# Half-array tiles for the second MLP product, four strips for the KV product, one half-array pair for the memory readout, in an infini-attention and mixer-MLP kernel

## The chip, the cores and the metric

The kernel runs on one core of one Trainium2 chip. The time is device microseconds of one execution of the whole program. TensorE (PE in the profile) multiplies and writes the accumulators in PSUM, which has eight banks; VectorE (DVE) and ScalarE (ACT) read them; GpSimd (POOL) works on SBUF alone; SyncE (SP) issues most of the DMAs.

## The reference

Two branches read the same normalised input and are added to it. With `x` of 2048 tokens by 512 features, 32 heads of 16, four segments of 512 tokens, and an MLP of 1792 hidden features:

```
xn = layernorm(x)
q, k, v = xn@wq, xn@wk, xn@wv              # 32 heads, 4 segments s
for s in segments:
    p     = softmax(q_s k_s^T * scale + mask)   # mask: -1e9 for keys after the query
    a_dot = p v_s
    a_mem = (phi(q_s) M) / (phi(q_s) z + 1e-6)  # phi(t) = t+1 or exp(t)
    o_s   = g*a_mem + (1-g)*a_dot               # g = sigmoid(beta), one per head
    M += phi(k_s)^T v_s ;  z += sum over tokens of phi(k_s)
out = x + o@wo + ( gelu(layernorm(xn)@w1 + b1)@w2 + b2 )
```

## The kernel before

The attention runs in 16 units `i`: four segments `s` by four groups `g` of eight heads (128 features). The MLP runs in 16 jobs `j`: eight blocks of 256 tokens (`hf`) by two halves of the hidden features (`fh`, `FH` = 7 chunks of 128). Most products are split into fp16 high and low parts, so that three fp16 matmuls stand for one (`split3`, L457, and the loops at L757 and L776). Every step is a key such as `("M", i, n)`; `streams()` lists the keys of each kind in their own order, and the string `ORDER` gives, letter by letter, from which list the next key is taken. Nothing reorders afterwards: each engine works through its instructions in that order, and an instruction whose semaphores are not there yet holds up what stands behind it on its engine. So `ORDER`, a table written out by hand or by a program, sets what lies between what.

The steps that matter here, with the lines that the profile shows:

- `T` (`qk_proj`, L457): projects q or k of one unit; the result goes through DRAM (`qd`, `kd`) into `qst`, `kst`, where heads lie on 48 rows from partitions 0 and 64.
- `M` (`m_jobs`, L580): q k^T for the row maxima; each step issues matmuls in pairs, one on array rows 0 to 47 and one on rows 64 to 111, into two PSUM banks. DVE takes the maxima (L587). There are 12 steps in a unit.
- `S` (`s_jobs`, L620): the logits again, transposed, in pairs on 50 rows each; ACT takes the exponent (L625), POOL masks (L634).
- `pv`, `PV` (`pv`, L649): fp32 probabilities times values, in four strips of 32 array columns that run side by side.
- `K` (`kv`, L556): phi(k)^T v, four fp32 products of 128 by 128, then masked to the heads' own blocks into `mst` (DVE L559, L563; POOL L564); the sum `z` comes from an accumulator output of L494 into `zst` (L561).
- `Z`, `Qd`, `Q` (`z_rep`, `a_mem`): L520 spreads `z`; one fp32 product for the denominators (L528), a reciprocal by ACT and DVE (L530, L507, L508, L512, L513), one fp32 product for the numerators (L536), multiplied in L537.
- `D` (`d_jobs`, L457), `G`, `H`: the first MLP product, GELU, and the split of the hidden part into `hT`.
- `e`, `E` (`e_jobs`, L757): the second MLP product. For each of two blocks `a` of 128 tokens, seven chunks of three full 128x128 fp16 matmuls add up in the bank `eacc`; then DVE adds the bank to `acc` (L761).
- `out` (L776, L779): the product with `wo`.

PSUM is divided in two: seven banks that all steps share (`dps`, tile `dense`) and one for `eacc` (`eps`). A transpose (L442, L501, L595) uses a shared bank too.

The array stands in one of three tilings in this program: full (128 rows by 128 columns), two halves of 64 rows (`M` and `S`), and four strips of 32 columns (`pv`). Read along PE's instructions, the tiling changes 412 times.

Of the kernel before, what the change touches and what calls it, by code (L numbers as in the profile page):

```python
# [57 lines left out]
def streams():  # L58
# [47 lines left out]
    "aacactutacttuaeuuutcccavecevvvaatcvcctvbwwvactwdvvwwftvttvxtxxbvytcxbvtwxcgcbxwxywxxhooobycxxsgycoiyziyizyonyo"  # L106
    "ciiyzzoypniizpniApifpnAqziqiiqqqzAzoimzzAzoozpoAoosjijqijjiqsjjioAiikkckkbihijqjsijijcqjiijqbqiqpfkbqkkakpmAAA"
    "ojAlqgjljojjqajlhookkkAkipiojopisjjiqjijqjipqiBqqiiBiAfoaqiikkkBkqqpqipgqmqspqlBphoqjljmjojiqiajqliojsiaikakkk"
    "ipiBqaqqjjjqoqjooajiqajioaisiibqfbpqkkkkqibqplqqpbgBpqhqlqmojjoqjjoojlioijiqkkipkkiBqjijqojijqqjjioqiipkkkkBli"
    "ifmnilnmlnbgrjjrjbjsrjijqqipiniikskkkipqqjijrjjiqjoiiqjikkkpkmlmioolhiofmqqoqpsjjmqjjgjjlqookbkkkmmsbjijijqqij"  # L110
    "ijiojiskikkkoplqiqholaiiifqmioqpomiqspgpqopqqaqqajjjqqomjiqjijqliqaqiikkipkkopiaajipshqoqijqjijpqijqqijaqopiqk"
    "kkaklqqomaoloaqqjbjfmoqbjsjjlqqmjbgkkkkbmmjjqojjqojiiojopibikkpkkpiiolnpiilhnqiiifqmilnompibngrjmjjjrjjsohipik"
    "kkskipirmjijrjiqjijqijqqqiipkkkkliiqqosqlqoiflomqoopqjjmsqjjgjjoombkkpkkqbqjmjiiqjqjijiqisjqqpsipkkkkiqqliqlho"
    "qqiiaifqmioomiqplgoqppmsaaoqjjjsqqomqjijqiqjiaoikikpakkqipqjiqqijqajoajjjohqqiikkkkpoalipiqqlooiaooaqbpmfqlbjm"
    "jjjqqjjqgbkkkkmbjjjqqoojibjqimjpqqqiikkkkplibiqolfinqiipnliimnpiomiogrojjmjsrjjoiipnjiqiikskkkiirjijqqijqjijqi"
    "jripkkkkiplqplfsqqoolqqmqojjjqmjjgojomkpkkksojqjjijqijiqiqpqjiosisikkpkqkbqlqilfisqqbiiiqpqmooipomqmgqqojjojjq"
    "ojqjliiiikkkkpijpoijiqjjiqjiijqikkiqpsqikkpqqqplplooqojqjjojjqqjlmokkkkqpqjjqjjqoojqjpqqkkkkqqplmqqqqqpqppqqqq"
    "lqqqqlqqqqrrqrr"
# [3 lines left out]
def plan():  # L122
# [3 lines left out]
    for c in "".join(ORDER):  # L126
        key = next(todo[NAMES.index(c)])
        k = key[0]
        need = "G" if k == "G" else "E" if k in ("S", "Qd") or k == "O" and key[2] == 0 or k == "T" and (
            key[1] >= NG if key[2] == 0 else key[1] < NU - NG) else tab  # L130
        yield key, None if need == tab else need
        tab = need
# [3 lines left out]
def infini_mixer_kernel(ctx: ExitStack, tc: tile.TileContext, x, wq, wk, wv, wo, beta, w1, b1, w2, b2, out):  # L136
# [9 lines left out]
    dps = ctx.enter_context(tc.tile_pool(name="dps", bufs=7, space=PSUM))  # L146
    eps = ctx.enter_context(tc.tile_pool(name="eps", bufs=1, space=PSUM))
# [315 lines left out]
    mst = cst.tile([P, NG, P], F32, name="mst")  # L463
    zst = cst.tile([P, NG], F32, name="zst")
    zs = {}

    def qk_proj(i, which):
# [19 lines left out]
        if phi:  # L487
            V.tensor_scalar(e, e, 1.0, qkcol(3, 1 - which, g), op0=OP.min, op1=OP.mult)
            if which == 0:
                V.scalar_tensor_tensor(e, p, 0.0, e, op0=OP.max, op1=OP.add)  # L490
            else:
                if s:
                    zs[i] = sm.tile([P, 1], F32, name="zs")
                V.scalar_tensor_tensor(e, p, 0.0, e, op0=OP.max, op1=OP.add,  # L494
                                       accum_out=zs[i] if s else zst[:, g:g + 1])
# [21 lines left out]
    def z_rep(i):  # L517
        g = i % NG
        zrt[i] = sm.tile([P, P], F32, name="zr", bufs=1)
        V.tensor_scalar(zrt[i], bd.rearrange("p a b -> p (a b)"), zst[:, g:g + 1], None, op0=OP.mult)  # L520
# [3 lines left out]
    def a_mem(i, part):  # L524
        g = i % NG
        p = dense()
        if part == 0:
            T.matmul(p, zrt[i], pqt[i, 0], start=True, stop=True)  # L528
            rd = sb.tile([P, 512], F32, name="rc")
            A.activation(rd, p, AF.Copy, bias=1e-6, scale=qkcs[:, 0, g:g + 1])  # L530
            ame[i] = sb.tile([P, 512], F32, name="ame")
            log_recip(rd, ame[i])
            newton(rd, rd, ame[i])
            rden[i] = rd
        else:
            T.matmul(p, mst[:, g, :], pqt[i, 0], start=True, stop=True)  # L536
            V.scalar_tensor_tensor(ame[i], p, bg[:, g, 4:5], rden[i], op0=OP.mult, op1=OP.mult)  # L537
# [13 lines left out]
    def kv(i):  # L551
        s, g = divmod(i, NG)
        p = dense()
        for b in range(4):
            v = vt[s, b][:, 4 * g:4 * g + 4, :].rearrange("p a (b c) -> p a b c", b=3)[:, :, 0:3:2, :]
            T.matmul(p[:, :P], pkn[i][:, b, :], v, start=b == 0, stop=b == 3)  # L556
        m = bd.rearrange("p a b -> p (a b)")
        if s == 0:
            V.tensor_tensor(mst[:, g, :], p[:, :P], m, op=OP.mult)  # L559
            return  # L560
        V.tensor_tensor(zst[:, g:g + 1], zs[i], zst[:, g:g + 1], op=OP.add)  # L561
        zr = sm.tile([P, P], F32, name="zr", bufs=1)
        V.tensor_tensor(zr, p[:, :P], m, op=OP.mult)  # L563
# [312 lines left out]
```

## Time and profile before

| | |
|---|---|
| median of 3 runs | 771.83 us (767.83 to 774.05) |
| span of the profiled execution | 772.1 us |
| busy: PE, DVE, ACT, POOL | 735.6, 541.2, 528.1, 352.3 us |
| second MLP product (L757) | 672 matmuls, 174.1 us busy |
| memory readout (L528, L536) | 48 fp32 matmul passes, 25.1 us busy |
| KV product (L556) | 96 fp32 matmul passes, 13.3 us busy |

The profiled execution lies within the range of the timed runs. A busy share is an average over the start, where weights are loaded and split, a long middle, and a tail with the last MLP block and the output product. An fp32 matmul shows as two passes in the trace. In the trace's rows in order of time, neighbouring instructions of one line are merged: the first number is the start, the second the length, which for PE includes the time that the last result needs to run out of the array; so the time that PE is held by a row is the start of the next row less its own.

### The profile page before, as it was taken

What the parts mean: (1) busy time and instruction counts of PE and PEld (TensorE: products, weight loads), DVE (VectorE), ACT (ScalarE), POOL (GpSimd) and SP (SyncE); (2) the same over time, 40 slices, a digit from 0 to 9 for tenths busy, and PEclk for the clock granted to TensorE, in tenths of its full rate; (3) what the DMA queues carried; (4) which work ended last, traced back from release to release, by engine and by line L of the source; (5) the groups of instructions that cost most, each with busy time, mean ns of one, the idle gap of its engine ahead of it and who ended that gap; (6) DMA issues with size and microseconds to landing.
All of it is one profiled execution on the core that took longest, in us unless ns stands there. A gap on an engine that the chain in (4) does not pass through costs nothing.

```text
span 772.1 us, 14761 instructions
## 1 busy us (share of the span) xinstructions
PE 735.6 (95%) x5301; PEld 384.0 (50%) x5301; DVE 541.2 (70%) x1677; ACT 528.1 (68%) x908; POOL 352.3 (46%) x544
## 2 busy tenths in 40 slices
PE   5889999999999998999999999999999999999997
PEld 4653545455544454555554454454554444453543
DVE  5788868879684857899486675979567673958332
ACT  5878788776885567576873948657784578666960
POOL 4465646544523533445544444354534244334651
PEclk9999999999999999999999999999999999998999
DMA  6874314142204223211312315140221314230001
GB/s 202 248 226 138 104 38 103 44 97 62 65 7 132 56 58 97 56 56 44 90 49 53 86 53 127 35 91 29 71 70 42 97 35 105 48 78 16 2 1 55
DMA packets 54085, 59.17 MB, mean 77 GB/s; under 512 B 5038, under 2 KB 40892, under 8 KB 54012
## 3 DMA queue, kind: packets, MB, share of 16 engines
q1 hardware_dynamic: 51708, 54.04, 24.8%
q0 software_dynamic: 2304, 4.20, 3.5%
q8 instruction: 41, 0.67, 0.4%
q14 instruction: 32, 0.26, 0.1%
HBM read 41.18 MB, written 17.04 MB: 75 GB/s over the span
## 4 chain that ended last, share of the span: by engine, by line
PE 69%; DMA 11%; ACT 8%; DVE 7%; issue 3%; POOL 2%; SPq 1%; ACTq 0%; DVEq 0%; POOLq 0%
PE dense L457 27%; PE eacc L757 15%; PE dense L649 8%; PE dense L580 5%; PE dense L776 4%; PE dense L620 4%; DMA qd<-hl 4%; DMA qst<-qd 4%; ACT pt L625 3%; PE dense L528 1%; PE dense L442 1%; DVE dense L587 1%; DMA w2s<-in_B_w_dram 1%; DVE hl L479 1%; ACT hl L475 1%
## 5 line engine op out<-in xcount | busy, mean ns | idle before, releaser
L587 DVE CUSTOM_DVE_ANT_0 dense<-dense,mask 128x512 f32<-128x512 f32 (+3 forms) x512 | 241.2, 515 | 24.3 <-PE dense L580 17.8
L625 ACT ACTIVATE pt<-dense,qkcs 128x512 f32<-128x512 f32 (+1 forms) x384 | 203.8, 627 | 30.6 <-PE dense L620 28.6
L757 PE MATMUL eacc<-w2s,hT 128*128 128x512 f16 x672 | 174.1, 385 | 2.0 <-DVE acc L761 1.9
L457 PE MATMUL dense<-yT,w1s 128*128 128x256 f16 x1344 | 162.4, 273 | 4.3 <-DVE yT L446 2.9
L634 POOL TENSOR_SCALAR_AFFINE_SELECT pt<-pt 128x256 f32<-128x256 f32 x256 | 101.4, 421 | 130.1 <-ACT pt L625 129.5
L457 PEld LDWEIGHTS <-w1s 128*128 128x128 f16 x1344 | 128.5, 98 | 36.5 <-issue 11.4
L730 POOL TENSOR_TENSOR hT<-hh,hT 128x512 f16<-128x512 f32 x64 | 66.5, 1039 | 90.0 <-ACT hT L729 87.2
L757 PEld LDWEIGHTS <-hT 128*128 128x128 f16 x672 | 58.0, 98 | 80.0 <-issue 31.7
L649 PE MATMUL dense<-pt,vt 128*32 128x512 f32 (+3 forms) x1024 | 78.0, 439 | 0.7 <-POOL hh L728 0.5
L580 PE MATMUL dense<-kst,qst 48*128 48x512 f16 (+3 forms) x512 | 66.9, 305 | 8.1 <-DMA qst<-qd 5.2
L587 DVE DVE_READ_ACCUMULATOR2_ANT mc<- 128x1 f32 x512 | 72.1, 141 | 0.0
L479 DVE SCALAR_TENSOR_TENSOR hl<-dense,hl 128x512 f16<-128x512 f32 x32 | 22.1, 689 | 65.3 <-ACT phq L478 41.5
L620 PE MATMUL dense<-qst,kst 50*128 50x512 f16 (+3 forms) x512 | 64.4, 302 | 2.7 <-ACT pt L625 2.0
L728 POOL TENSOR_SCALAR hh<-hT,sc 128x512 f32<-128x512 f32 x64 | 42.8, 669 | 36.3 <-ACT hT L721 34.2
L729 ACT ACTIVATE hT<-hh 128x512 f16<-128x512 f32 x64 | 36.6, 572 | 32.5 <-POOL hh L728 32.4
L714 ACT ACTIVATE hT<-dense,b1t,sc 128x256 f32<-128x256 f32 x64 | 36.2, 566 | 23.8 <-PE dense L457 23.2
L649 PEld LDWEIGHTS dense<-pt,vt 128*32 128x32 f32 x1024 | 29.6, 110 | 44.7 <-issue 34.4
L580 PEld LDWEIGHTS <-qst 48*128 48x128 f16 x512 | 22.1, 95 | 51.9 <-issue 36.1
L475 ACT ACTIVATE hl<-dense 128x512 f16<-128x512 f32 x32 | 19.0, 595 | 41.4 <-PE dense L457 41.4
L679 POOL TENSOR_TENSOR nN<-nN,oT 128x512 f32<-128x512 f32 x16 | 20.3, 1269 | 56.9 <-DVE oT L513 56.9
L620 PEld LDWEIGHTS <-kst 50*128 50x128 f16 x512 | 21.4, 94 | 46.8 <-issue 39.8
L457 PE MATMUL dense<-xnT,wks 128*128 128x512 f16 x192 | 44.3, 379 | 0.4 <-DVE xnT L446 0.3
(225 smaller groups left out, 1034.9 us busy)
## 6 DMA issues: line engine op xcount, KB each, us to landing
xt<-in_A_x_dram SPq DMA_DIRECT2D x30, 256.0 KB
kd<-hl SPq DMA_DIRECT2D x48, 128.0 KB
kst<-kd SPq DMA_DIRECT2D x32, 192.0 KB
qd<-hl SPq DMA_DIRECT2D x48, 128.0 KB
qst<-qd SPq DMA_DIRECT2D x32, 192.0 KB
acc<-in_A_x_dram SPq DMA_DIRECT2D x16, 256.0 KB
acc<-in_B_b_dram POOLq DMA_DIRECT2D x16, 256.0 KB, 4.4
out_dram<-acc SPq DMA_DIRECT2D x16, 256.0 KB
```

Of the source, the lines that this page charges most:

```text
L457: T.matmul(p, wsl(ws, k, a), xsl(xs, k, b), start=s0 and i == 0, stop=s1 and i == 3 * n - 1)
L580: T.matmul(p[:, o:o + n], stk[i, 0][r, t, P * qb:P * qb + P], stk[i, 1][r, t, :n], start=True, stop=True)
L587: V.tensor_tensor_reduce(p[:, o:o + n], p[:, o:o + n], mask[:, 512 - n:], 1.0, -3e38, OP.add, OP.max, mc[i][:, 4 * b + t, qb:qb + 1])
L620: T.matmul(p[:, o:o + n], stk[i, 1][r, t, P * kb:P * kb + P], stk[i, 0][r, t, P * kb:], start=True, stop=True)
L625: A.activation(e[:, OFF[kbs[0]]:OFF[kbs[0]] + o], p[:, :o], AF.Exp, scale=qkcs[:, 1, i % NG:i % NG + 1])
L634: G.affine_select(v, v, pattern=[[0, 2], [1, P]], compare_op=OP.is_ge, fill=0.0, base=0, channel_multiplier=-1)
L649: T.matmul(p[32 * c:32 * c + 32, P * kb:], vt[s, kb][:, 4 * g + c, 16 * odd:16 * odd + 32], pt[i, 2 * c + odd][:, OFF[kb]:OFF[kb] + LEN[kb ...
L714: A.activation(hz[:, fi, :], p[:, :256], AF.Identity, bias=b1t[:, fo:fo + 1], scale=col(CG + fh))
L728: G.tensor_scalar(t, hz[:, z, :], col(SHH + j % 2), 0.0, op0=OP.mult, op1=OP.add)
L729: A.activation(hT[:, z, 0, :], t, AF.Copy)
L730: G.tensor_tensor(hT[:, z, 1, :], t, hT[:, z, 0, :], op=OP.subtract)
L757: T.matmul(p, t[:, u, P * a:P * a + P], w2s[:, fo, v, :], start=fi == 0 and n == 0, stop=fi == FH - 1 and n == 2)
```

## The change

- **Second MLP product.** `e_jobs` becomes `e_part(j, n)`, 14 steps for a job. Both token blocks of the job add up at once, in two banks (`pes[j]`). Each 128-row product is cut into two 64-row ones on the two halves of the array; in steps 0 to 6 the upper half works for block 0 and the lower for block 1, in steps 7 to 13 the other way round. After step 6 a copy of one element by DVE (`fence`) reads the bank, and the first matmul into it in step 7 waits for that read. At step 13 DVE adds both banks to `acc`.
- **KV product.** `kv` multiplies in four strips of 32 columns, each with the 48 columns of `vt` for two heads: value, ones, value. The ones give `z`, so `zst`, `zs`, the accumulator output of L494 and two mask steps go; `mst` holds 48 columns instead of 128, and one DVE instruction adds them.
- **Memory readout.** `z_rep` builds one matrix with four DVE instructions; `a_mem` part 0 multiplies once, as a pair of 64-row fp32 halves into two banks, which gives numerators and denominators together; ACT and DVE read each bank once. Part 1 does the reciprocal and one POOL product.
- **Banks.** One ring of eight `dense` banks; a job of the second MLP product holds two of them from its step 0 to its step 13.
- **Order.** A new string `ORDER`.

```
-        for a in range(2):
-            if fh == 0:
-                accs += [("A", 2 * hf + a, k) for k in range(2)]
-            mlp += [("e", j, a, f) for f in range(FH - 1)] + [("E", hf, a, fh)]
+        if fh == 0:
+            accs += [("A", 2 * hf + a, k) for a in range(2) for k in range(2)]
+        mlp += [("e", j, n) for n in range(2 * FH)]
...
-    "aacctutacttuaeuuutcccavecevvvaatcvcctvbwwvactwdvvwwftvttvxtxxbvytcxbvtwxcgcbxwxywxxhooobycxxsgycoiyziyizyonyo"
+    "aeatcctcutcuettcctcvvvatuaatuacevcaaabcvvbccwtvucwvfbtdvbtwvtvxtxxvyxwxxgwxcxyxxhtoooxywocwoosyyniyyzoiyccziigps"
...
-    dps = ctx.enter_context(tc.tile_pool(name="dps", bufs=7, space=PSUM))
-    eps = ctx.enter_context(tc.tile_pool(name="eps", bufs=1, space=PSUM))
+    dps = ctx.enter_context(tc.tile_pool(name="dps", bufs=8, space=PSUM))
...
     def z_rep(i):
-        V.tensor_scalar(zrt[i], bd.rearrange("p a b -> p (a b)"), zst[:, g:g + 1], None, op0=OP.mult)
+        t = zrt[i] = sm.tile([P, P], F32, name="zr", bufs=1)
+        for b in range(2):
+            r = slice(64 * b, 64 * b + 64)
+            m = bd[r, 4 * b:4 * b + 4, :].rearrange("p (c o) e -> p c o e", o=2)
+            w = mst[r, g, :].rearrange("p (k e) -> p k e", k=3)
+            for own, src in ((True, w[:, 0:3:2].unsqueeze(1)), (False, w[:, 1:2].unsqueeze(1))):
+                c = 64 * (b if own else 1 - b)
+                V.tensor_tensor(t[r, c:c + 64].rearrange("p (c o e) -> p c o e", c=2, o=2), m,
+                                src.broadcast_to([64, 2, 2, DH]), op=OP.mult)
...
         if part == 0:
-            T.matmul(p, zrt[i], pqt[i, 0], start=True, stop=True)
+            ps = dense(), dense()
+            for b, p in enumerate(ps):
+                r = slice(64 * b, 64 * b + 64)
+                T.matmul(p, zrt[i][r], pqt[i, 0][r], start=True, stop=True)
...
+            for b, p in enumerate(ps):
+                r, z = slice(64 * b, 64 * b + 64), slice(64 - 64 * b, 128 - 64 * b)
+                A.activation(rd[r], p[z], AF.Copy, bias=1e-6, scale=qkcs[r, 0, g:g + 1])
+                V.tensor_scalar(n[r], p[r], bg[r, g, 4:5], None, op0=OP.mult)
         else:
-            T.matmul(p, mst[:, g, :], pqt[i, 0], start=True, stop=True)
-            V.scalar_tensor_tensor(ame[i], p, bg[:, g, 4:5], rden[i], op0=OP.mult, op1=OP.mult)
+            rd = rden[i]
+            t = sb.tile([P, 512], F32, name="rt")
+            log_recip(rd, t)
+            newton(rd, rd, t)
+            G.tensor_tensor(ame[i], ame[i], rd, op=OP.mult)
...
         for b in range(4):
-            v = vt[s, b][:, 4 * g:4 * g + 4, :].rearrange("p a (b c) -> p a b c", b=3)[:, :, 0:3:2, :]
-            T.matmul(p[:, :P], pkn[i][:, b, :], v, start=b == 0, stop=b == 3)
+            for c in range(4):
+                T.matmul(p[32 * c:32 * c + 32, :48], pkn[i][:, b, 32 * c:32 * c + 32], vt[s, b][:, 4 * g + c, :],
+                         start=b == 0, stop=b == 3, tile_position=(0, 32 * c), skip_group_check=True)
...
+    def e_part(j, n):
         hf, fh = divmod(j, 2)
+        ph, fi = divmod(n, FH)
+        if n == 0:
+            pes[j] = dense(), dense()
+        fo = FH * fh + fi
+        for m, (u, v) in enumerate(((0, 0), (0, 1), (1, 0))):
+            for b in range(2):
+                a = b ^ ph
+                r = slice(64 * b, 64 * b + 64)
+                T.matmul(pes[j][a], hTs[fh][r, fi, u, P * a:P * a + P], w2s[r, fo, v, :],
+                         start=n == 0 and m == 0, stop=fi == FH - 1 and m == 2, skip_group_check=True)
+        if n == FH - 1:
+            V.tensor_copy(fence, pes[j][1][:1, :1])
+        if n == 2 * FH - 1:
+            for a in range(2):
+                t = acc[2 * hf + a]
+                V.scalar_tensor_tensor(t, pes[j][a], col(C2 + fh), t, op0=OP.mult, op1=OP.add)
+                added(2 * hf + a)
```

How the order moves the work is best seen on PE, where unit 6's `M` steps, unit 5's `S` steps and job 4's second MLP product meet. Before (`kst`, `qst` are the operands of `M` and `S`, `eacc` is the second MLP product; each kind issues more rows of the same form, left out here):

```order
L580 MATMUL dense<-kst_94,qst_92 128x384
...
L580 MATMUL dense<-kst_94,qst_92 128x128
L620 LDWEIGHTS kst_95
L620 MATMUL dense<-qst_93,kst_95 128x256
...
L757 LDWEIGHTS hT_116
L757 MATMUL eacc<-w2s,hT_116 128x512
...
L580 LDWEIGHTS qst_92
L580 MATMUL dense<-kst_94,qst_92 128x256
```

Now the same place, with steps 6 and 7 of job 4 (`dense<-w2s` is now the second MLP product):

```order
L754 LDWEIGHTS hT_112
L754 MATMUL dense<-w2s,hT_112 128x512
...
L580 LDWEIGHTS qst_89
L580 MATMUL dense<-kst_91,qst_89 128x384
...
L580 MATMUL dense<-kst_91,qst_89 128x128
L620 LDWEIGHTS kst_92
L620 MATMUL dense<-qst_90,kst_92 128x256
...
L754 LDWEIGHTS hT_112
L754 MATMUL dense<-w2s,hT_112 128x512
```

Before, the run of full-array L757 rows stands between half-array rows, and the tiling changes on both sides of it; now all these rows are half-array rows. Over the whole program the changes of tiling on PE go from 412 to 250 (full to halves and back: 330 to 172; with strips on one side: 82 to 78).

On DVE at the same place of the changed kernel, the fence of job 4 stands behind the maxima of one `M` step:

```order
L503 SCALAR_TENSOR_TENSOR rc<-rc,rt 128x512
L564 TENSOR_TENSOR mst<-dense,mst 128x48
L587 ISA dense,mc<-dense,mask 128x512
L587 ISA mc 128x1
...
L757 COPY fence<-dense 1x1
L587 ISA dense,mc<-dense,mask 128x384
```

No such copy stood there before. Step 7's matmuls on PE wait for it, and what PE has between steps 6 and 7 here is one `M` step and one `S` step.

On PE around the readout of unit 4, before, there are two places for one unit, one for the denominators and one for the numerators, both between full-array rows:

```order
L457 MATMUL dense<-xnT,wks 128x512
L528 MATMUL dense<-phq,zr 128x512
L457 LDWEIGHTS xnT
...
L457 MATMUL dense<-wvs,xnT 128x512
L536 MATMUL dense<-phq,mst 128x512
L457 LDWEIGHTS xnT
```

Now there is one place, between half-array rows:

```order
L620 MATMUL dense<-qst_90,kst_92 128x512
L528 MATMUL dense<-phq,zr 128x512 x2
L754 LDWEIGHTS hT_113
L754 MATMUL dense<-w2s,hT_113 128x512
```

SP's queue keeps its kinds of transfers. At the start, one pair of `xt` loads now stands ahead of the `w1s` loads instead of behind them, and the two remaining `w1s` loads stand together.

More of the change, by code (lines that the diff above doesn't have):

```diff
@@ L105 @@
 ORDER = (
[L106 to L115, printed above, removed]
@@ L488, in qk_proj @@
             V.tensor_scalar(e, e, 1.0, qkcol(3, 1 - which, g), op0=OP.min, op1=OP.mult)
[L489 to L495, printed above, removed]
+            V.scalar_tensor_tensor(e, p, 0.0, e, op0=OP.max, op1=OP.add)
             pqt[i, which] = e
```

72 lines of the change are left out of this document (23 added, 49 removed).

## The prediction

> **What bounds the kernel now.** First the head of the page and its forty slices:
>
> ```profile
> PE 735.6 (95%) x5301; PEld 384.0 (50%) x5301; DVE 541.2 (70%) x1677; ACT 528.1 (68%) x908; POOL 352.3 (46%) x544
> ...
> PE   5889999999999998999999999999999999999997
> ...
> DVE  5788868879684857899486675979567673958332
> ```
>
> PE is full in nearly every slice but the first three. The busy time by stage says the same in figures (stretch, PE, PEld, DVE, ACT, POOL, then clock and DMA):
>
> ```profile
> 0.00:100.00 100.00, 81.48 (x574) 50.70 (x575) 76.08 (x265) 75.32 (x136) 56.05 (x76) 0.98 0.61 177
> 100.00:700.00 600.00, 588.25 (x4321) 304.08 (x4319) 437.27 (x1351) 412.83 (x707) 264.35 (x421) 1.00 0.26 67
> ```
>
> From 100 to 700 us PE is busy for 588.25 of 600 us; DVE has 73% and ACT 69%. So in this stage time taken off PE is time taken off the kernel, as long as nobody else becomes late. The waits of PE show how little it waits for today (total, times, longest):
>
> ```profile
> PE dense L580 <- DMA qst<-qd: 5.2, 7, 1.8
> ...
> PE dense L620 <- ACT pt L625: 2.0, 6, 0.8
> PE eacc L757 <- DVE acc L761: 1.9, 3, 0.8
> ...
> PE dense L580 <- ACT pt L625: 0.6, 3, 0.2
> ```
>
> But a busy PE need not be multiplying. Rows in order of time, each held until the next one starts:
>
> ```profile
> 640.38 0.82 PE L757 MATMUL eacc<-w2s,hT 128*128 128x512 f16 x3
> 641.04 1.02 PE L536 MATMUL dense<-phq,mst 128*128 128x512 f32 x2
> 641.99 0.55 PE L620 MATMUL dense<-qst,kst 50*128 50x512 f16 x3
> ...
> 647.12 0.28 PE L620 MATMUL dense<-qst,kst 50*128 50x256 f16 x2
> 647.34 1.49 PE L457 MATMUL dense<-yT,w1s 128*128 128x256 f16 x12
> 648.75 2.36 PE L649 MATMUL dense<-pt,vt 128*32 128x512 f32 x32
> 651.04 1.48 PE L457 MATMUL dense<-yT,w1s 128*128 128x256 f16 x12
> ...
> 655.52 0.82 PE L757 MATMUL eacc<-w2s,hT 128*128 128x512 f16 x3
> 656.28 0.39 PE L580 MATMUL dense<-kst,qst 48*128 48x384 f16 x4
> ...
> 656.93 0.82 PE L757 MATMUL eacc<-w2s,hT 128*128 128x512 f16 x3
> 657.69 0.57 PE L580 MATMUL dense<-kst,qst 48*128 48x512 f16 x2
> ```
>
> Three L757 matmuls take 641.04 - 640.38 = 0.66 us when another full-array row follows (0.22 each), but 656.28 - 655.52 = 0.76 and 657.69 - 656.93 = 0.76 us when a half-array row follows. **A change of tiling costs 0.10 us.** It costs as much on the way back: the L620 pair at 647.12 has 256 columns, 0.11 us at the pace above, and holds PE for 0.22.
>
> **The change, part by part.** The sum is made against the profiled execution's 772.1 us; the median of the runs is 771.83, so both stand for the same.
>
> *Changes of tiling.* They fall from 412 to 250, counted along PE's instructions (a transpose with few outputs counted as full array). 162 x 0.10 us = **-16.2 us**, 14.6 to 17.8 with the 0.01 that two decimals leave open. Nothing covers them today, since PE is the engine that is waited for.
>
> *Second MLP product.* 672 full matmuls become 1344 half ones, in 672 pairs.
>
> ```profile
> L757 PE MATMUL eacc<-w2s,hT 128*128 128x512 f16 x672 | 174.1, 385 | 2.0 <-DVE acc L761 1.9
> L580 PE MATMUL dense<-kst,qst 48*128 48x512 f16 x128 | 30.4, 389 | 6.5 <-DMA qst<-qd 5.2 <-DVE mc L587 0.3 <-DVE hT L716 0.3
> ...
> 242.65 0.61 PE L620 MATMUL dense<-qst,kst 50*128 50x512 f16 x6
> 243.19 2.12 PE L776 MATMUL dense<-wos,oT 128*128 128x512 f16 x9
> ```
>
> The three L620 pairs at 242.65 have 512, 384 and 128 columns, 1024 in all; they hold PE for 0.54 us, of which 0.10 is the change behind them, so 0.44 us: 0.22 for 512 columns, what one full matmul takes. So a pair costs what it replaces: **0**. Upper bound by the rows' mean, 389 against 385 ns: 672 x 4 ns = +2.7 us.
>
> *Memory readout.* Twelve units, two fp32 products each before, one pair now.
>
> ```profile
> 227.78 1.02 PE L528 MATMUL dense<-phq,zr 128*128 128x512 f32 x2
> 228.63 2.75 PE L457 MATMUL dense<-wvs,xnT 128*128 128x512 f16 x12
> ```
>
> One product holds PE for 0.85 us. If the two halves run side by side, as the fp16 halves do and as the fp32 strips at 648.75 do, one product of the two goes: 12 x 0.85 = **-10.2 us**. No row shows fp32 on half arrays, so the other bound is 0. I take the full gain, since the strips are fp32.
>
> *KV product.* Eight passes of 128 columns before, eight groups of four strips with 48 columns now, twelve units.
>
> ```profile
> 153.84 1.05 PE L556 MATMUL dense<-vt,pkn 128*128 128x128 f32 x8
> 154.72 1.46 PE L757 MATMUL eacc<-w2s,hT 128*128 128x512 f16 x6
> ...
> 664.70 0.43 PE L649 MATMUL dense<-pt,vt 128*32 128x128 f32 x8
> ```
>
> Before: 0.88 us a unit, 0.11 a pass. A group of four strips with 128 columns is also at most 0.11 (two groups in 0.43 us with a run-out; the 32 strips at 648.75, 2560 columns in all groups, take 2.29 less 0.10, or 0.11 for 128 columns). At the same pace 48 columns are 0.04. So 0.33 us a unit if columns set it, 0.88 if a group cannot go faster than with 128: -6.6 to 0. No row has so few columns. I take **-4 us**, nearer the columns, since every strip row so far goes by its columns.
>
> The Trainium skill, page "TensorEngine Tiling (Array Packing)", section "Instruction Overhead", speaks against this part: a matmul has an overhead of about 60 cycles, and one column takes as long as 60. By it, with 60 columns at the rows' pace (0.025 us) as an estimate, a unit's 32 strip passes one behind the other would be 0.8 us, a gain of 1 us over the twelve units instead of 4, and the total would be 750 us. The strip rows say that the overhead is not paid four times in a group, but none is this short.
>
> *Fence and banks.* Sixteen new round trips PE, DVE, PE. The nearest row is the wait for DVE at the reuse of `eacc`:
>
> ```profile
> 747.06 5.30 PE L757 MATMUL eacc<-w2s,hT 128*128 128x512 f16 x21 [0.84 <-DVE acc L761]
> ```
>
> Uncovered it costs 0.84 us. Before there are 31 such round trips and 1.9 us of waits: the order puts other PE work between. Between steps 6 and 7 of the sixteen jobs there now stand, at the rows' prices (0.11 to 0.22 us for an `M` or `S` pair, 1.3 for a `D`, 2.3 for `pv`), 0.5, 2.0, 1.1, 0.3, 0.3, 0.7, 5.0, 0.5, 3.8, 4.0, 4.1, 3.0, 5.9, 2.8, 2.3 and 0 us. Only the last is bare: +0.84. Behind a step 7 that waits stand all later matmuls, since PE is in order. On DVE the copy waits for step 6, and the next maxima (L587) stand behind it; DVE's free 27% takes that. The 1.9 us of today's `eacc` waits go. While a job runs, the ring has six banks for everything else, where there were seven; PE's waits for L625 today come to 2.6 us. I let the tighter ring add twice that and the short covers one microsecond: 0.8 + 1 - 1.9 + 5.2, **+5 us**, -2 (nothing but the `eacc` waits changes) to +14 (each of the seven covers under 1.2 us fails by 0.84 us, and the ring's waits are four times today's).
>
> *Other engines.*
>
> ```profile
> L537 DVE SCALAR_TENSOR_TENSOR ame<-dense,bg,rc 128x512 f32<-128x512 f32 x12 | 9.0, 747 | 6.8 <-PE dense L536 5.5 <-POOL hT L730 0.9 <-PE dense L595 0.4
> L716 DVE TENSOR_SCALAR hT<-dense,sc,b1t 128x256 f32<-128x256 f32 x48 | 25.9, 539 | 24.2 <-PE dense L457 24.2
> L520 DVE TENSOR_SCALAR zr<-bd,zst 128x128 f32<-128x128 f32 x12 | 3.9, 321 | 1.1 <-POOL mst L564 1.1
> L563 DVE TENSOR_TENSOR zr<-dense,bd 128x128 f32<-128x128 f32 x8 | 2.3, 285 | 1.8 <-PE dense L556 1.7
> L530 ACT ACTIVATE rc<-dense,qkcs 128x512 f32<-128x512 f32 x12 | 8.3, 691 | 2.3 <-PE dense L528 2.3
> L681 POOL TENSOR_TENSOR nN<-nN,ame 128x512 f32<-128x512 f32 x12 | 15.2, 1267 | 0.9
> ```
>
> A unit of the readout loses L537 (0.75 us) on DVE and gains two reads of a bank, each between L716 (0.54) and L537 (0.75); `Z` goes from 0.32 to four small ones, at most 0.29 each like L563; `K` loses about 0.3. That is about +1 us x 12 on DVE with the fences inside the rounding: 541 to some 553. ACT gains one L530 a unit, 8 us; POOL one product like L681, 15 us, less the additions to `mst`. All that lies beside PE, which still has the most work (some 706 us): **0**. If that cover were gone, DVE's 12 us would show.
>
> *Start.* SP's queue takes one pair of `xt` loads (512 KB) ahead of `w1s`; at the 177 GB/s of the first stage that is 3 us later for `w1s`, while PE has warm-up matmuls and the weight splits ahead. I take **0**, -3 to +3.
>
> Sum: 772.1 - 16.2 - 10.2 - 4 + 5 = 746.7, **747 us**.
>
> **The rivals.**
>
> *The gain is stopped by DVE.* Six of forty slices of DVE show 9, ten show 8. If the gain of 25 us is lost in the first and halved in the second, 11/40 x 25 = 7 us are missing, and 16/40 of DVE's added 12 us lie bare, 5 us: 759 us. For it: ACT and DVE also grow while PE shrinks. Against: in the middle stage DVE has 27% free, and the waits above give little time to it.
>
> *The fence meets a late DVE.* This one ends slower. DVE can be far behind PE:
>
> ```profile
> 405.66 0.72 PE L580 MATMUL dense<-kst,qst 48*128 48x256 f16 x8
> 406.31 2.76 PE L457 MATMUL dense<-xnT,wks 128*128 128x512 f16 x12
> ...
> 410.74 0.14 DVE L587 DVE_READ_ACCUMULATOR2_ANT mc<- 128x1 f32 x1
> ```
>
> Those eight `M` matmuls were through at 406.31, their last maximum at 410.88: 4.6 us. A fence stands behind such maxima in DVE's order. With 4.6 us at each fence less the cover above, the sixteen cost 39 us: 747 + 39, less the 2 already counted, is 784 us. It decides from 1.6 us a fence on (25 us over sixteen). For it: six covers under 1.2 us. Against: 31 round trips cost 1.9 us today.
>
> *The small-matmul parts bring nothing.* The fp32 halves run one after the other and the strips keep the pace of 128 columns: 747 + 10 + 4 = 761 us. For it: no row of either. Against: strips and fp16 halves do overlap.
>
> **How the numbers follow.** Forecast 0.64, DVE stop 0.14, late fence 0.12, small parts 0.10. The forecast's own case lies wholly under 764 us, the line of 1% (about what a measurement of this kernel can tell from no change). Of the DVE stop and of the small parts some two thirds lie under it, one third within 1%. That is 0.64 + 0.16 = 0.80 faster, 0.08 the same, 0.12 slower. The range's lower end takes the best of every part: 772.1 - 17.8 - 10.2 - 6.6 - 2 - 3 = 732.5, taken as 732 us. Its upper end, 769 us, holds both rivals on the fast side and the forecast with +14 for fences and banks; what lies above is the late fence.
>
> **What would show it.** Right: a three-pair group of the second MLP product between `M` and `S` rows holds PE 0.65 us, and such groups touch half-array rows without the 0.10; L528 has one row of four passes in 0.85 to 0.95 us; the KV row under 0.6 us; PE busy near 706 us, and PE's waits on the fence and on L587 and L625 together under 8 us. Wrong: pairs slower than 0.22 us; waits of the second MLP product on DVE of a microsecond or more, job after job; slices in which DVE stands at 9 while PE falls to 8.

## The result and the profile after

The changed kernel takes **747.41 us** (median of four runs, 746.63 to 747.67) against 772.1 us for the kernel before in the same job: a ratio of 0.9702, 95% interval [0.9662, 0.9742]. Four runs more, in a later job, gave 746.47 us and 0.9672 [0.9617, 0.9727]. The forecast was 747.0.

The head of the page after (busy time, the slices of PE and DVE, the chain that ended last):

```profile
PE 708.0 (95%) x6261; PEld 397.7 (53%) x6261; DVE 562.7 (75%) x1721; ACT 536.1 (72%) x920; POOL 365.3 (49%) x548
...
PE   7899998999999999899999999989999999999997
...
DVE  6789878978884877978688677989478575969233
...
PE 47%; DVE 32%; ACT 7%; issue 5%; POOL 5%; DMA 2%; POOLq 0%; DVEq 0%; SPq 0%; ACTq 0%
```

PE's busy time fell from 735.6 to 708.0 us and DVE's rose from 541.2 to 562.7. PE is still full in nearly every slice, but the chain that ended last now goes through DVE for 32% (7% before). In slice 17 DVE stands at 9 while PE falls to 8, which is the sign the prediction named for its DVE rival, in one slice of forty.

The same stages as before (stretch, PE, PEld, DVE, ACT, POOL, clock, DMA):

```profile
0.00:100.00 100.00, 88.87 (x686) 55.40 (x688) 80.20 (x269) 79.68 (x145) 56.00 (x77) 0.93 0.61 177
100.00:700.00 600.00, 578.87 (x5256) 324.05 (x5253) 468.63 (x1432) 435.90 (x743) 289.61 (x444) 1.00 0.25 67
```

In the middle PE was free for 11.8 of 600 us before (600 - 588.25) and is free for 21.1 us now. So the kernel became faster although PE waits more. What it waits for (total, times, longest):

```profile
PE dense L595 <- DVE mc L587: 4.3, 6, 1.5
...
PE dense L580 <- DVE mc L587: 2.7, 7, 0.5
...
PE dense L620 <- DVE mc L587: 1.6, 4, 0.7
...
PE dense L455 <- ACT pt L625: 1.4, 1, 1.4
...
PE dense L595 <- DVE fence L757: 0.2, 1, 0.2
PE dense L754 <- DVE fence L757: 0.2, 1, 0.2
```

The wait for the q transfers (5.2 us before) is gone. The waits of PE that end with one of the sixteen fences come to 0.4 us together. The maxima of the `M` groups (L587) have become its main releaser.

The rows of PE that the prediction asked for, in order of time (start, busy):

```profile
639.73 1.02 PE L754 MATMUL dense<-w2s,hT 64*128 64x512 f16 x6
640.39 0.52 PE L580 MATMUL dense<-kst,qst 48*128 48x384 f16 x3
...
640.83 1.01 PE L754 MATMUL dense<-w2s,hT 64*128 64x512 f16 x6
641.48 0.64 PE L620 MATMUL dense<-qst,kst 50*128 50x384 f16 x3
```

```profile
183.78 0.55 PE L559 MATMUL dense<-vt,pkn 128*32 128x48 f32 x32
184.15 1.04 PE L649 MATMUL dense<-pt,vt 128*32 128x512 f32 x8
...
197.47 1.02 PE L528 MATMUL dense<-phq,zr 64*128 64x512 f32 x4
198.33 0.81 PE L754 MATMUL dense<-w2s,hT 64*128 64x512 f16 x6
...
420.99 0.52 PE L559 MATMUL dense<-vt,pkn 128*32 128x48 f32 x32
421.33 1.04 PE L649 MATMUL dense<-pt,vt 128*32 128x384 f32 x12
```

Three pairs of the second MLP product, with half-array rows on both sides, hold PE for 640.39 - 639.73 = 0.66 and 641.48 - 640.83 = 0.65 us: the price of three full matmuls, with no change of tiling behind. The KV unit holds it 0.34 and 0.37 us in the two rows shown, with other strips behind it (0.88 before), the readout pair 0.86 us in one row of four passes (two products of 0.85 before).

**Where the 26.6 us went.** From the start times of all matmuls of a trace, the time from the first to the last can be split in three: the columns that the program streams, at the 0.216 us per 512 columns at which full-array matmuls follow one another in both traces (median of some 180 intervals of the output projection); the changes of tiling, at the 0.097 us they take in both; and the rest, which is waiting, short matmuls that don't reach that pace, and stretches at half clock.

| kernel | first to last | columns | changes of tiling | rest |
|---|---|---|---|---|
| before | 766.3 | 658.1 | 412: 39.9 | 68.3 |
| after | 739.7 | 641.4 | 250: 24.2 | 74.1 |
| difference | -26.6 | -16.7 | -15.7 | +5.8 |

The granted clock is 0.990 over both executions, so the difference is not the clock. The prediction had -14.2 for the columns (readout and KV), -16.2 for the changes and +5 for fence and banks. In total and in its parts the sum came out. Whether each part is *worth* its size is another question, and the experiments answer it otherwise.

### The profile page after: what moved, and what is told of

It reads as the page before. It is cut to its first block, busy times and chain, and to the rows that moved or that the text cites. A ratio compares the mean times of both kernels' runs of the same rounds, so it can differ in the third digit from the quotient of the medians.

```text
span 745.9 us, 16734 instructions
## 1 busy us (share of the span) xinstructions
PE 708.0 (95%) x6261; PEld 397.7 (53%) x6261; DVE 562.7 (75%) x1721; ACT 536.1 (72%) x920; POOL 365.3 (49%) x548
## 4 chain that ended last, share of the span: by engine, by line
PE 47%; DVE 32%; ACT 7%; issue 5%; POOL 5%; DMA 2%; POOLq 0%; DVEq 0%; SPq 0%; ACTq 0%
PE dense L455 20%; DVE dense L587 13%; PE dense L754 7%; PE dense L649 6%; PE dense L773 4%; PE dense L620 3%; PE dense L580 3%; DVE mc L587 3%; ACT pt L625 2%; DVE hl L475 2%; PE dense L786 1%; PE dense L440 1%; DVE oT L502 1%; DVE zr L517 1%; DVE phk L484 1%
## 5 line engine op out<-in xcount | busy, mean ns | idle before, releaser
L587 DVE CUSTOM_DVE_ANT_0 dense<-dense,mask 128x512 f32<-128x512 f32 (+3 forms) x512 | 240.6, 516 | 25.1 <-PE dense L580 18.2
L625 ACT ACTIVATE pt<-dense,qkcs 128x512 f32<-128x512 f32 (+1 forms) x384 | 207.6, 623 | 43.0 <-PE dense L620 38.1
L754 PE MATMUL dense<-w2s,hT 64*128 64x512 f16 x1344 | 177.3, 376 | 0.6 <-POOL hT L730 0.2
L455 PE MATMUL dense<-yT,w1s 128*128 128x256 f16 x1344 | 160.6, 273 | 6.3 <-DVE mhl L598 1.8
L455 PEld LDWEIGHTS <-w1s 128*128 128x128 f16 x1344 | 128.2, 98 | 39.2 <-issue 18.8
L754 PEld LDWEIGHTS <-hT 64*128 64x128 f16 x1344 | 71.0, 94 | 62.0 <-issue 12.8
L580 PE MATMUL dense<-kst,qst 48*128 48x128 f16 (+3 forms) x512 | 72.3, 297 | 6.4 <-DVE mc L587 2.7
L620 PE MATMUL dense<-qst,kst 50*128 50x512 f16 (+3 forms) x512 | 72.4, 298 | 5.2 <-DVE mc L587 1.6
L587 DVE DVE_READ_ACCUMULATOR2_ANT mc<- 128x1 f32 x512 | 72.1, 141 | 0.2
L649 PEld LDWEIGHTS dense<-pt,vt 128*32 128x32 f32 x1024 | 32.1, 109 | 42.2 <-issue 32.3
L620 PEld LDWEIGHTS <-kst 50*128 50x128 f16 x512 | 27.3, 94 | 38.7 <-issue 23.8
L580 PEld LDWEIGHTS <-qst 48*128 48x128 f16 x512 | 28.3, 94 | 35.7 <-issue 21.4
L455 PE MATMUL dense<-xnT,wqs 128*128 128x512 f16 x192 | 46.6, 395 | 0.1
L455 PE MATMUL dense<-xnT,wks 128*128 128x512 f16 x192 | 46.6, 395 | 0.1
```

What stands on the lines that cost most here:

```text
L455: T.matmul(p, wsl(ws, k, a), xsl(xs, k, b), start=s0 and i == 0, stop=s1 and i == 3 * n - 1)
L580: T.matmul(p[:, o:o + n], stk[i, 0][r, t, P * qb:P * qb + P], stk[i, 1][r, t, :n], start=True, stop=True)
L587: V.tensor_tensor_reduce(p[:, o:o + n], p[:, o:o + n], mask[:, 512 - n:], 1.0, -3e38, OP.add, OP.max, mc[i][:, 4 * b + t, qb:qb + 1])
L620: T.matmul(p[:, o:o + n], stk[i, 1][r, t, P * kb:P * kb + P], stk[i, 0][r, t, P * kb:], start=True, stop=True)
L625: A.activation(e[:, OFF[kbs[0]]:OFF[kbs[0]] + o], p[:, :o], AF.Exp, scale=qkcs[:, 1, i % NG:i % NG + 1])
L649: T.matmul(p[32 * c:32 * c + 32, P * kb:], vt[s, kb][:, 4 * g + c, 16 * odd:16 * odd + 32], pt[i, 2 * c + odd][:, OFF[kb]:OFF[kb] + LEN[kb ...
```

## The experiments

Times are medians of four runs each unless another count stands beside them; ratios are to the kernel before on the same chip.

**1. Second MLP product back in full-array matmuls**, with the order, the banks and the copies as changed. The copy now reads a bank that is finished, so no matmul waits for it any more.

```diff
-            for b in range(2):
-                a = b ^ ph
-                r = slice(64 * b, 64 * b + 64)
-                T.matmul(pes[j][a], hTs[fh][r, fi, u, P * a:P * a + P], w2s[r, fo, v, :], ...)
+            T.matmul(pes[j][ph], hTs[fh][:, fi, u, P * ph:P * ph + P], w2s[:, fo, v, :], ...)
...
-            V.tensor_copy(fence, pes[j][1][:1, :1])
+            V.tensor_copy(fence, pes[j][0][:1, :1])
```

> The changed kernel with its order, its banks and its fence copies, but the second MLP product in full-array matmuls again (steps 0 to 6 for one token block, 7 to 13 for the other; the fence reads a finished bank, so no matmul waits for it). Changes of tiling on PE go from 250 to 498, the multiplying itself stays the same. Theory 1, PE's held time sets the end: 248 x 0.096 = 23.8 us more than 747.4, so 771 us. Theory 2, DVE now sets a good part of the middle: PE has slack there, about half shows, so 759 us.

Measured: 754.01 us, 0.9775 [0.9737, 0.9814]: 6.6 us more than the changed kernel (7.5 against the later four runs of it), less than either theory. Its head and its middle stage:

```profile
PE 720.5 (96%) x5589; PEld 367.4 (49%) x5589; DVE 561.7 (75%) x1721; ACT 536.9 (71%) x920; POOL 365.9 (49%) x548
```

```profile
100.00:700.00 600.00, 586.52 (x4648) 295.15 (x4641) 464.68 (x1424) 429.53 (x729) 283.06 (x434) 1.00 0.25 67
```

There are 498 changes of tiling here, 24.1 us more of them than in the changed kernel, and the rest falls from 74.1 to 55.9 us: PE is free for 13.5 us in the middle instead of 21.1. Of the 18 us by which the rest falls, 14 are time at matmuls behind which PE waits (59 such places instead of 91), and 5 are half clock, which this execution had less of (0.998 granted against 0.990). So more than half of the 24 us fill time in which PE would have waited anyway. Half arrays and fence together are worth 6.6 us in this order by the medians; the four executions here were granted 0.996 on average and those of the changed kernel 0.992, which may hide some 3 us more.

**2. The readout's pair issued twice**, so that the saved product is paid again.

```diff
-            for b, p in enumerate(ps):
-                r = slice(64 * b, 64 * b + 64)
-                T.matmul(p, zrt[i][r], pqt[i, 0][r], start=True, stop=True)
+            for _ in range(2):
+                for b, p in enumerate(ps):
+                    r = slice(64 * b, 64 * b + 64)
+                    T.matmul(p, zrt[i][r], pqt[i, 0][r], start=True, stop=True)
```

> The changed kernel with the fp32 pair of the readout issued twice into the same banks (the second overwrites the first with the same values): nothing else changes, on no other engine. It puts back exactly the PE time that the pair saved, 12 x 0.86 = 10.3 us. Theory 1 (PE sets the end): 757.7 us. Theory 2 (DVE sets a good part): 752 us or less.

Measured: 749.47 us, 0.9713 [0.9675, 0.9752]: +2.1 us (+3.0 against the later four runs) for 10.4 us more on PE (PE is busy 714.8 us against 708.0), the second theory's side. The rest falls to 66.8. Again only a fifth to a third of PE's time shows; the interval overlaps that of the changed kernel, so the share is rough.

**3. The changed code in the old order.** Only the table `ORDER` is that of before.

```diff
-    "aeatcctutcuettcctcvvvatuaatuacevcaaabcvvbccwtvucwvfbtdvbtwvtvxtxxvyxwxxgwxcxyxxhtoooxywocwoosyyniyyzoiyccziigps"
...
+    "aacactutacttuaeuuutcccavecevvvaatcvcctvbwwvactwdvvwwftvttvxtxxbvytcxbvtwxcgcbxwxywxxhooobycxxsgycoiyziyizyonyo"
...
```

> The changed code with the order string of before. Changes of tiling 351 (before 412, changed kernel 250). Theory 1, the parts add up on PE whatever the order: 772.1 - 61 x 0.096 - 10.2 - 6.5 (KV as the trace after shows it) = 749.6 us. Theory 2, the order carries the gain, since the two banks held by a job and the fence meet work that was not arranged for them: 760 us or more, with new waits of PE for DVE and ACT. The start should tell too: if the earlier start of unit 1's M steps (9 us earlier in the trace after) comes from the order, it is missing here.

Measured: 811.69 us, 1.0523 [1.0468, 1.0578]. The first theory missed by 62 us. It has 351 changes of tiling, 5.9 us less of them than before, the same columns as the changed kernel, and a rest of 125.2 us: in the old order PE waits. The granted clock is 0.977. Of the 40 us by which it is slower than before, the new KV product and readout alone bring 21 in that order (run 4); the other 19 come with the half arrays, their fence and the accumulators in the ring, and no run takes these three apart.

**4. New KV product and readout alone**, in the kernel before, with its order, its seven banks and `eacc`, and full-array second MLP product (433 changes of tiling).

```diff
-    mst = cst.tile([P, NG, P], F32, name="mst")
-    zst = cst.tile([P, NG], F32, name="zst")
+    mst = cst.tile([P, NG, 48], F32, name="mst")
...
-            T.matmul(p[:, :P], pkn[i][:, b, :], v, start=b == 0, stop=b == 3)
+            for c in range(4):
+                T.matmul(p[32 * c:32 * c + 32, :48], pkn[i][:, b, 32 * c:32 * c + 32], vt[s, b][:, 4 * g + c, :], ...)
```

> Before's order, banks and second MLP product, with the new KV product and readout alone. Changes of tiling 433. Theory 1: 772.1 + 21 x 0.096 - 10.2 - 6.5 = 757.4 us. Theory 2 (these parts move work to DVE, ACT and POOL, and the gain is lost there): 765 us or more.

Measured: 793.07 us, 1.0298 [1.0241, 1.0355]: slower than before, though its columns take 16.7 us less. The waits that had grown, on PE, DVE and POOL:

```profile
PE dense L581 <- DMA qst<-qd: 13.9, 12, 2.6
...
PE eacc L752 <- DVE acc L756: 4.7, 4, 3.3
```

```profile
POOL ame L541 <- DVE rc L504: 33.5, 12, 7.8
```

The q transfers come late (5.2 us of waiting before), and POOL now stands 33.5 us at the readout's product, behind DVE's reciprocal. That last wait need not cost anything: in the changed kernel POOL stands there for 37.2 us (`POOL ame L540 <- DVE rc L503: 37.2, 12, 6.9`), and it is the faster one. Part of the loss is the clock: its mean is 0.976 of a span of 788.9 us, which is 18.9 us of granted clock missing; before it is 0.990 of 772.1 us, 7.7 us.

**5. The same with the reciprocal in its early place.** The readout moved `log_recip` and `newton` from the entry that makes the denominators to the entry that uses them; here they go back.

```diff
...
             for b, p in enumerate(ps):
...
+            t = sb.tile([P, 512], F32, name="rt")
+            log_recip(rd, t)
+            newton(rd, rd, t)
         else:
             rd = rden[i]
-            t = sb.tile([P, 512], F32, name="rt")
-            log_recip(rd, t)
-            newton(rd, rd, t)
             G.tensor_tensor(ame[i], ame[i], rd, op=OP.mult)
```

> The kernel before with its order, its banks and its second MLP product, the new KV product and the new readout, as in the run of that combination (793.1 us, POOL waiting 33.5 us for DVE's reciprocal at the readout's multiply, the M group waiting 13.9 us for the q transfers); but the logarithm, Newton step and exponential of the denominators go back from the readout's own entry to the earlier entry that makes the denominators, as before. Number of instructions and tiling changes as in that run. Theory 1 (what the new parts lost in the old order was lost because the reciprocal moved to just before its use, so that POOL and DVE stand in order behind it): most of the loss goes, 768 us or less, and POOL's wait at that multiply falls under 10 us. Theory 2 (the loss comes from the added reads of the doubled readout and of the replicated denominators on ACT and DVE, which are all still there): 785 us or more.

Measured: 787.23 us, 1.0217 [1.0131, 1.0303]. POOL's wait at that product falls from 33.5 to 7.9 us, but only 5.8 us come back, within the overlap of the two intervals. The first theory, mine until then, had 768 us or less and falls: moving the reciprocal back does not bring back the loss. It doesn't show either that its place cost nothing, since one wait was exchanged for another: PE waits less for the q transfers (10.3 us, 13.9 in run 4) and for the accumulator (1.9, 4.7 in run 4), but 10.8 us instead of 2.7 for the maxima. What PE waits for there:

```profile
PE dense L596 <- DVE mc L588: 10.8, 6, 2.5
PE dense L581 <- DMA qst<-qd: 10.3, 11, 3.2
```

**6. And the replicated denominators on POOL**, on top of run 5.

```diff
-                V.tensor_tensor(t[r, c:c + 64].rearrange("p (c o e) -> p c o e", c=2, o=2), m, ...)
+                G.tensor_tensor(t[r, c:c + 64].rearrange("p (c o e) -> p c o e", c=2, o=2), m, ...)
```

> The combination of the new KV product and the new readout in the order of before, with the reciprocal in its early entry (787.2 us), and the 48 products that replicate the denominators moved from DVE to POOL (13.6 us off DVE). Theory 1 (this combination is slower than before because DVE, with 16 us more work than before, is late for the M groups' reductions and the q transfers): most of the 15 us comes back, 777 us or less. Theory 2 (it is slower because the pair of the readout holds two banks of the ring at an earlier place, where before held one): 784 us or more.

Measured: 781.18 us, 1.0149 [1.0071, 1.0227], between the two theories: another 6.0 us for some 10 us less on DVE (547.6 us busy against 557.2). The steps of runs 4, 5 and 6 point one way, but neighbouring intervals overlap. The 9 us by which the last is still slower than before stay open: its pair of banks is taken early, its accumulator waits and its order are those of before, and no run takes these apart.

**7. The same products on POOL, in the changed kernel.**

```diff
-                V.tensor_tensor(t[r, c:c + 64].rearrange("p (c o e) -> p c o e", c=2, o=2), m, ...)
+                G.tensor_tensor(t[r, c:c + 64].rearrange("p (c o e) -> p c o e", c=2, o=2), m, ...)
```

> The changed kernel with the 48 products that replicate the denominators (13.6 us of DVE, 0.32 us each) issued on POOL instead of DVE; nothing else differs. Theory 1 (PE alone sets the end, DVE's added work is covered): 747 us, within 1. Theory 2 (the chain through DVE sets a third of the end, as the chain of waits shows, so that time off DVE comes off the kernel in part): 740 to 744 us. Rival (POOL, which is slower at such products and stands in order behind the readout, becomes late): over 750 us, with new waits of PE or ACT on POOL.

Measured: 745.75 us, 0.9662 [0.9603, 0.9722]. **8. One eviction of the first MLP product per job moved from DVE to ACT as well.**

```diff
-Z_ON = "AVAVAVA"
+Z_ON = "AVAAAVA"
```

> The changed kernel with the 48 replicating products on POOL (745.8 us) and one of the three evictions per job of the first MLP product that DVE makes moved to ACT as well: 16 x 0.54 = 8.6 us off DVE, as much onto ACT. Theory 1 (DVE holds the banks longest, so what leaves it frees banks): 743 to 745 us. Theory 2 (ACT, 72% busy, is as tight): 746 us or more.

Measured: 745.46 us, 0.9654 [0.9601, 0.9708]. **9. The changed kernel once more beside it.**

> The changed kernel itself once more, beside the others on this chip: 746.6 to 748 us, so that a difference of under 1 us between two variants is read as none.

Measured: 746.47 us (745.0 to 748.03). DVE is busy 551.3 us in run 7 and 544.1 in run 8, against 562.5 in run 9: 18 us less DVE work brings 1 us, which is within the spread of the runs. The work isn't gone but moved: POOL is busy 380.1 us in run 8 against 365.4, ACT 542.8 against 536.2, and PE now waits 2.2 us for POOL's products. Neither variant is shown to beat the changed kernel.

**10. DVE work added at the fences.** The copy of one element becomes a maximum over the bank.

```diff
-    fence = cst.tile([1, 1], F32, name="fence")
+    fence = cst.tile([P, 1], F32, name="fence")
...
-            V.tensor_copy(fence, pes[j][1][:1, :1])
+            V.tensor_reduce(fence, pes[j][1], axis=AX.X, op=OP.max)
```

> The changed kernel in which each of the 16 fence copies (one element, 0.146 us) becomes a maximum over the whole bank (128x512, about 0.6 us by the reductions of the M groups at the same place), so some 7 us more on DVE at just the points where PE may be held; the bank is left as it was. Theory 1 (DVE has slack at the fences, since PE waits for them 0.2 us in all): 747 to 749 us. Theory 2 (the fences sit where DVE sets the pace): 7 us more, 754 us.

Measured: 750.45 us, 0.9719 [0.9658, 0.978]. The row of the fences on DVE, 0.145 us each in the changed kernel:

```profile
L757 DVE TENSOR_REDUCE fence<-dense 128x1 f32<-128x512 f32 x16 | 11.0, 688 | 10.5 <-PE dense L754 10.4
```

8.7 us more DVE work right where the second MLP product waits for it costs 3.0 to 4.0 us against the two medians of the changed kernel. Neither theory's number: most of the delay is covered even there.

**11. Seven banks in the ring** of the changed kernel, and **12. six in that of the kernel before** (which has `eacc` besides).

```diff
-    dps = ctx.enter_context(tc.tile_pool(name="dps", bufs=8, space=PSUM))
+    dps = ctx.enter_context(tc.tile_pool(name="dps", bufs=7, space=PSUM))
```

> The changed kernel with seven banks in the ring instead of eight; nothing else differs. Theory 1 (the ring has slack, banks are free well before their next turn): 747 to 749 us. Theory 2 (the freeing of banks by ACT and DVE is what holds PE in the middle, so the eighth bank carries part of the gain): 755 us or more, with the bank waits of M, KV and the first MLP product growing.

```diff
-    dps = ctx.enter_context(tc.tile_pool(name="dps", bufs=7, space=PSUM))
+    dps = ctx.enter_context(tc.tile_pool(name="dps", bufs=6, space=PSUM))
```

> The kernel before with six banks in its ring instead of seven, the accumulator's own bank kept; nothing else differs. The changed kernel with one bank fewer lost 30.5 us. Theory 1 (both orders use the ring to its end, a bank in the ring is what lets PE run ahead of DVE and ACT): 15 to 45 us more, 787 to 817 us. Theory 2 (only the changed order needs eight, since its accumulators now sit in the ring; before had a bank to spare): 772 to 776 us.

Measured: 777.88 us (10 runs), 1.0074 [1.0044, 1.0105], for the changed kernel with one bank less, so **+30.5 us**; 795.0 us, 1.0307 [1.0247, 1.0366], for the kernel before with one less, **+23.2 us**. With either order left as it is, one bank weighs about as much as the whole gain of 24.7 us; whether another order would win part of it back was not run. In the changed kernel with seven banks PE's waits begin:

```profile
PE dense L455 <- DVE mc L587: 6.2, 9, 2.2
PE dense L455 <- DVE mhl L598: 3.9, 1, 3.9
PE dense L580 <- DVE mc L587: 3.6, 10, 0.6
PE dense L455 <- DVE nD L663: 3.3, 3, 1.2
```

```profile
100.00:700.00 600.00, 565.16 (x5014) 318.48 (x5014) 447.72 (x1362) 413.94 (x706) 272.47 (x418) 0.99 0.25 66
```

L455 here is the projections and the first MLP product. They read nothing that the maxima (L587) write, so a wait of L455 on L587 is a wait for a bank. All waits of L455 together go from 6.5 to 22.4 us, all of PE's from 31.3 to 49.8. The other 12 us of the loss are in a busier PE (721.2 us for the same 6261 matmuls), and most of that is waiting too, since the profile counts a wait only from the moment at which the last result has run out of the array. Counted from start to start, as in the table above, the rest grows by 32.7 us, from 74.1 to 106.8: 26 of them at matmuls behind which PE waits (138 such places instead of 91), 2.5 from half clock.

## Why the prediction was right, and where not

**Changes of tiling.** Forecast -16.2 us, measured -15.7: 162 fewer at 0.097 us. Right.

**Second MLP product.** Forecast 0: three pairs in 0.65 to 0.66 us. Right. But the step said that nothing covers the changes, "since PE is the engine that is waited for". Run 1 puts them back, and more, and most of them are covered. So -15.7 us is the size of this term in the accounting of the whole change, not what the half arrays bring by themselves; in the final order that is 6.6 us by the medians.

**Readout.** Forecast -10.2 us: the row of four passes holds 0.86 us where two products held 0.85 each, so the fp32 halves do run side by side and the rival in which they don't is out. The term is right as PE time; run 2 says that 2 to 3 us of it reach the end.

**KV product.** Forecast -4, measured some -6.5 us: 12 x (0.88 - 0.34), with no change of tiling behind either. The columns set it, as the better of the two bounds (-6.6) had it; the choice of a value between the bounds mis-sized this term. The Trainium skill, page "TensorEngine Tiling (Array Packing)", section "Instruction Overhead", gives each matmul an overhead of about 60 cycles. The prediction's estimate from it, 0.8 us for a unit, does not agree with the rows of 0.34 and 0.37 us: the passes of a group are not paid one behind the other.

**Fence and banks.** Forecast +5, made of 0.8 for a bare fence, 1 for short covers, -1.9 for `eacc` and +5.2 for the tighter ring. The rest grew by 5.8 us, but differently. Waits for fences come to 0.4 us. The ring was sized from 2.6 us of waits for L625, and that reasoning does not hold: with these same small waits in the kernel before, taking one bank away costs 23 us (run 12). What a bank is worth could not be read from PE's waits. That +5 stands so near to +5.8 is luck. The accumulators could move into the ring for so little only with the new order: in the old one the rest is some 100 us without half arrays and accumulators in the ring (run 4) and 125.2 us with them (run 3).

**Other engines.** DVE grew by 21.5 us, not 12. Its rows:

```profile
L534 DVE TENSOR_SCALAR ame<-dense,bg 64x512 f32<-64x512 f32 x24 | 18.0, 749 | 15.7 <-POOL nN L681 8.2 <-ACT rc L533 4.9 <-POOL pt L634 1.8
L517 DVE TENSOR_TENSOR zr<-bd,mst 64x64 f32<-64x64 f32 x48 | 13.6, 321 | 0.2
```

Each half-height read of a bank takes 0.749 us, as much as the full-height L537 did, the upper end of the bounds, and the four small products take 0.321 us each, above the 0.29 that I allowed. It made little difference: in runs 7 to 9, moving 18 us off DVE brought about 1 us. So the DVE rival, 759 us, did not happen, though its signs (waits on L587, 32% of the chain) are in the profile. PE's waits on fences, L587 and L625 come to 12 us, where under 8 was forecast.

**Start.** Forecast 0. Unit 1's first `M` row starts at 79 us instead of 87, and unit 2's at 125 instead of 129, so some 4 us were gained by then. The new code in the old order (run 3) has them at 88 and 131, so the earlier start comes with the order. How much of it reaches the end no run shows.

**The late fence**, the rival on the slower side, priced a fence at up to 4.6 us less its cover. Sixteen fences brought 0.4 us of waits. The bare one, in the last job, holds PE for 0.64 us from the last pair ahead of it (724.69 us) to the first behind it (725.33 us); 0.22 of that are columns, so it cost 0.42 us where the sum had 0.84. Even 0.54 us more work in each (run 10) brings under 4 us. The covers that the prediction listed from the order were enough.

**The step that failed** without showing in the number is the first one: "time taken off PE is time taken off the kernel". In the final order, time added to PE counts for a fifth to two fifths (runs 1 and 2, with the clock's share left open), time moved off DVE for less than a tenth where it is spread (runs 7 and 8), time added to DVE at the fences for less than a half (run 10), and a bank for 30 us. These are the worths at the changed kernel; what the first microseconds taken off the kernel before brought was not measured. My reading is that PE, DVE, ACT and the ring are tight together: added work on one of them fills the holes that the others leave. That reading fits all runs; it is not shown by one that takes the mechanism itself away. In the old order the same parts made the kernel slower (runs 3 and 4). So the sum came out because the change brought an order that keeps the rest near 70 us, and the prediction had no term for that: this much of its being right is luck. The reverse, the old code in the new order, wasn't run, so how much the order would bring by itself stays open.

## What to carry to other kernels

A profile with one engine at 95% can still have a second bound: take one buffer of a ring away before relying on the busy share, since a bank was worth 23 to 30 us here, and PE's waits for L587 and L625, which free banks, came to 6 us in the kernel before and 12 in the changed one. A saving that is counted in engine time holds for the order that goes with it; the same matmuls saved in an order fitted to other code made the kernel 3 to 5% slower. Small matmuls that use disjoint parts of the array run side by side, down to 48 columns of fp32, and putting half-array work next to half-array work saves 0.10 us of PE's time at each seam, of which the kernel's time shows only a part where PE waits anyway.

## What the hardware showed besides

A wait can cost more than its length. In the kernel before, a wait of 1.83 us for a q transfer is followed by a stretch at half the granted clock (the windows' columns as above, the clock ahead of the last two):

```profile
298.35 0.39 PE L580 MATMUL dense<-kst,qst 48*128 48x512 f16 x1 [1.83 <-DMA qst<-qd]
...
299.22 2.56 PE L757 MATMUL eacc<-w2s,hT 128*128 128x512 f16 x6
```

```profile
299.40:302.80 3.40, 3.40 (x13) 1.03 (x12) 2.54 (x13) 1.78 (x5) 1.53 (x4) 0.51 0.28 50
```

Six L757 matmuls take 2.56 us there, 1.46 elsewhere. After the first 50 us and up to the last matmul, stretches at half clock last 3.4 or 6.8 us in the traces. The kernel before has two of them, 10.2 us in all; the changed kernel has none; the new KV product and readout in the old order have six, 27.3 us. At half speed that is about 5, 0 and 14 us of PE's time, so some 9 us of the loss in run 4 are the clock. The gain of the change is not: in the first 50 us the changed kernel has 13.7 us at half clock and the kernel before 3.4, and over the whole both stand at 0.990. Single executions of the kernel before range from 0.982 (777.68 us) to 0.996 (767.75 us).

Not each wait does it, and not each stretch has a long wait ahead of it: in run 4 a wait of 2.57 us, up to 164.75 us, is followed by full clock, and in the kernel before a stretch of 6.8 us begins at 702.2 us, behind waits of 0.2 us. The stretches of a trace begin on a grid of 3.413 us. What separates the two kinds of windows of that grid, in the fourteen traces, is how much of the array was in use: the streaming time of the window's matmuls (the columns at the pace above), each weighted by the share of the 128 by 128 array that it uses, as a share of the window. After the first 50 us there are 2870 windows at full clock, and 29 are followed by half clock. All 26 windows under 0.36 are among them and none over 0.39; of the seven between, three are. The window ahead of 299.4 us has 0.26 and the one ahead of 702.2 us 0.37, with many small half-array matmuls in it; the grid cuts the wait of 2.57 us into two windows, the emptier of them at 0.365. The Trainium skill, page "TensorE: Matmul & The Clock Gate", Part 1, has the clock halved after an idle window of about 3.4 us on a free-running grid; the lengths agree with that grid, but a wait of 1.83 us is shorter than a window, and of the 29 windows ahead of a stretch one alone was idle throughout.
